# Decode attention: key chunks of 128 instead of 64, two-bank q·k sums, and A's output row as one 512-column strip

## The chip, the cores and the metric

The kernel runs on one core of a Trainium2 chip. The metric is the device time of one execution in microseconds (us). "PE" is the matmul engine, "DVE" VectorE, "ACT" ScalarE, "SP" the engine whose queue issues the loads; in the profile lines "PEld" is PE's loading of weights and "POOL" GpSimd. SBUF is the on-chip memory that holds the tiles, here over 128 partitions (128x8192 in the profile is 8192 elements in each); PSUM is the memory that PE sums into. A run's profile is of one of its executions, so its times belong to that execution alone. PE's granted clock is the share of full speed that the profile says it was given; in the records it is 0.50 or 1.00.

## The reference, cut to what matters

Two attention problems, A and B, one query token each, 32 heads of 128. A reads 16384 keys and values per head, B only the last 4096.

```
q      = x @ wq                                   # 512 -> 32 heads x 128
scores = einsum("bhqd,bhkd->bhqk", q, k) * 128**-0.5
p      = softmax(scores)
o      = einsum("bhqk,bhkd->bhqd", p, v)
out    = o.reshape(1, 1, 32 * 128) @ wo           # 4096 -> 512
# A: all 16384 keys; B: the last 4096; result: concatenate(a, b)
```

Every key and value is read once and used once: 335 MB of keys and values, 17 MB of weights.

## The kernel before

Keys come in loads of 8 MB (a tile of 128 partitions x 256 keys x 128 values, bf16; B's in two halves). DVE multiplies keys by q and folds the product once; PE sums on with identity matmuls; DVE reduces; ACT takes the exponential. All that goes by chunks of U keys.

```python
U = 64
KEYS = 256

def _mult(nc, cx, ch):                       # DVE: k *= q, in place
    ...
def _add(nc, cx, ch):                        # DVE: first half of d += second half
    k = ch.unit.load.kt[:, ch.k0 : ch.k0 + U, :]
    cx.o(nc.vector.tensor_tensor(
        out=k[:, :, 0 : DH // 2], in0=k[:, :, 0 : DH // 2], in1=k[:, :, DH // 2 : DH], op=ALU.add))

def _red(nc, cx, ch):                        # PE: 64 values -> 8, sums in PSUM
    W = 512 // U
    nb = DH // 2 // W
    ch.red = cx.red_pool.tile([P, U, W], F32, tag="red", name="red")
    for b in range(nb):
        cx.o(nc.tensor.matmul(ch.red[:, :, :], lhsT=cx.ident[:, :],
            rhs=ch.unit.load.kt[:, ch.k0 : ch.k0 + U, b * W : (b + 1) * W],
            start=(b == 0), stop=(b == nb - 1)))
    ...                                      # last chunk: the key buffer is free
```

The output rows come last. A's row of 512 is two strips of 256 columns (rows 0 and 32 of PSUM), B's likewise. PE works at two such strips together.

```python
def _out(nc, cx, st, j0, n):
    if j0 == 0:
        st.oc = ...                          # DVE copies the (P, J) columns out of PSUM
    w = st.DN // 2
    out = [o[r : r + 1, :] for o, r in zip(cx.out_ps, st.out_rows)]
    for j in range(j0, j0 + n):
        for x in range(2):
            cx.o(nc.tensor.matmul(out[x], lhsT=st.oc[:, j : j + 1],
                rhs=st.wo_t[:, j, x * w : (x + 1) * w], start=(j == 0), stop=(j == J - 1)))
    if j0 + n == J:
        ...                                  # DVE and ACT copy a half each; SP stores the row
```

The pools are laid out one after another in each SBUF partition:

```python
    cx.singles = pool("singles", 1)          # ident, place, csA, csB, masks, q, ...
    cx.small = pool("small", 1)
    cx.kt_pool = pool("kt", 2)               # two buffers of keys, 64 KB a partition each
    cx.vt_pool = pool("vt", 1)               # one buffer of values
    ...
    st.cs = cx.singles.tile([P, H, st.keys // U], F32, tag=f"cs{st.name}", name=f"cs{st.name}")
```

The softmax here doesn't subtract the row's maximum and nothing guards it: scores larger than these inputs give would overflow.

Of the kernel before, what the change touches and what calls it, by code (L numbers as in the profile page):

```python
# [8 lines left out]
F32 = mybir.dt.float32  # L9
BF16 = mybir.dt.bfloat16  # L10
P = 128
# [2 lines left out]
AX = mybir.AxisListType  # L14

DH = 128
U = 64
KEYS = 256
SCALE = 1.0 / math.sqrt(DH)

# [9 lines left out]
class _Order:  # L30


    def __init__(self, tc):
        self.tc = tc
# [27 lines left out]
class _Chunk:  # L62
    def __init__(self, unit, i):
        self.unit, self.i, self.k0 = unit, i, unit.k0 + i * U


class _Unit:


    def __init__(self, st, i, load, k0):  # L70
        self.st, self.i, self.R = st, i, st.R
        self.load, self.k0 = load, k0
        self.h0 = i * st.R
        self.chunks = [_Chunk(self, c) for c in range(st.keys // U)]
        self.stage = None
# [93 lines left out]
def _mult(nc, cx, ch):  # L169

    u = ch.unit
    k = u.load.kt[:, ch.k0 : ch.k0 + U, :]
    q = u.st.qall[:, u.i * DH : (u.i + 1) * DH]
    cx.o(nc.vector.tensor_tensor(  # L174
        out=k, in0=k,
        in1=q.rearrange("p (o d) -> p o d", o=1).broadcast_to([P, U, DH]),
        op=ALU.mult,
    ))


def _add(nc, cx, ch):
    k = ch.unit.load.kt[:, ch.k0 : ch.k0 + U, :]
    cx.o(nc.vector.tensor_tensor(  # L183
        out=k[:, :, 0 : DH // 2], in0=k[:, :, 0 : DH // 2], in1=k[:, :, DH // 2 : DH], op=ALU.add,
    ))


def _red(nc, cx, ch):
    W = 512 // U
    nb = DH // 2 // W  # L190
    ch.red = cx.red_pool.tile([P, U, W], F32, tag="red", name="red")
    for b in range(nb):
        cx.o(nc.tensor.matmul(  # L193
            ch.red[:, :, :],
            lhsT=cx.ident[:, :],
            rhs=ch.unit.load.kt[:, ch.k0 : ch.k0 + U, b * W : (b + 1) * W],
            start=(b == 0),
            stop=(b == nb - 1),
        ))
    if ch is ch.unit.load.chunks[-1]:  # L200
        cx.loads.release("kt")


def _softmax(nc, cx, ch):

    u = ch.unit
    R = u.R
    sc = cx.sc_pool.tile([P, U], F32, tag="sc", name="sc")
    cx.o(nc.vector.tensor_reduce(out=sc[:, :], in_=ch.red[:, :, :], axis=AX.X, op=ALU.add))  # L209
    ch.p = u.st.p_pool.tile([P, U // 4, R, 4], BF16, tag=f"p{u.st.name}", name="p_sb")  # L210
    for g in range(R):
        cx.o(nc.scalar.activation(  # L212
            out=ch.p[:, :, g, :],
            in_=sc[:, :].rearrange("p (t e) -> p t e", e=4),
            func=ACT.Exp,
            scale=SCALE,
            bias=u.st.off[:, g : g + 1],
            accum_out=u.st.cs[:, u.h0 + g, ch.i : ch.i + 1],
        ))
# [80 lines left out]
def _out(nc, cx, st, j0, n):  # L300
    J = st.wo.shape[0] // P
    if j0 == 0:
        st.oc = cx.singles.tile([P, J], BF16, tag=f"oc{st.name}", name=f"oc{st.name}")
        cx.o(nc.vector.tensor_copy(st.oc[:, :], st.oc_ps[:, 0:J]))  # L304
    w = st.DN // 2
    out = [o[r : r + 1, :] for o, r in zip(cx.out_ps, st.out_rows)]
    for j in range(j0, j0 + n):
        for x in range(2):
            cx.o(nc.tensor.matmul(  # L309
                out[x],  # L310
                lhsT=st.oc[:, j : j + 1],
                rhs=st.wo_t[:, j, x * w : (x + 1) * w],
                start=(j == 0),
                stop=(j == J - 1),
            ))
    if j0 + n == J:
        row = cx.accs_pool.tile([1, st.DN], BF16, tag="accs", name=f"row{st.name}")
        cx.o(nc.vector.tensor_copy(row[0:1, 0:w], out[0]))  # L318
        cx.o(nc.scalar.copy(row[0:1, w:], out[1]))
        cx.o(nc.sync.dma_start(out=cx.out[0, 0:1, st.at : st.at + st.DN], in_=row[0:1, :]))  # L320


# [1 line left out]
def kernel(  # L324
# [14 lines left out]
    nc = tc.nc  # L339
# [4 lines left out]
    cx = _Ctx()  # L344
    cx.o = _Order(tc)
    cx.out = out
    pool = lambda name, bufs, **kw: ctx.enter_context(tc.tile_pool(name=name, bufs=bufs, **kw))
# [3 lines left out]
    cx.kt_pool = pool("kt", 2)  # L351
    cx.vt_pool = pool("vt", 1)
    cx.accs_pool = pool("accs", 1)
    cx.sc_pool = pool("sc", 2)
    cx.p_poolA = pool("pA", 7)
    cx.p_poolB = pool("pB", 4)
    cx.red_pool = pool("red", 2, **PS)
    cx.psf_pool = pool("psf", 1, **PS)
    cx.pst_pool = pool("pst", 1, **PS)
# [5 lines left out]

    def problem(name, x, k_cache, v_cache, wq, wo, sk0, W, at):
        st = _Problem()
        st.name, st.x, st.wq, st.wo, st.at = name, x, wq, wo, at
        st.R, st.keys = (2, KEYS) if name == "A" else (4, KEYS // 2)
        assert st.R * W == P * st.keys  # L370
        st.DN = wo.shape[1]
        st.k_view = k_cache[0, :, sk0 : sk0 + W, :]
        st.v_view = v_cache[0, :, sk0 : sk0 + W, :]
        st.out_rows = (0, 32) if name == "A" else (64, 96)
        st.f_at = 0 if name == "A" else 32
        assert k_cache.shape[1] == 32
        st.p_pool = cx.p_poolA if name == "A" else cx.p_poolB
        n = KEYS // st.keys * st.R
        st.loads = [_Load(st, i) for i in range(k_cache.shape[1] // n)]
        st.units = [u for x in st.loads for u in x.units]  # L380
        return st

    stA = problem("A", A_x, A_k_cache, A_v_cache, A_wq, A_wo, 0, SkA, 0)
    stB = problem("B", B_x, B_k_cache, B_v_cache, B_wq, B_wo, SkB - WB, WB, A_wo.shape[1])

    loads = []
# [19 lines left out]
    for i, p in enumerate(pieces):  # L406
# [16 lines left out]
        out=cx.ident[:, :],  # L423
# [10 lines left out]
    w = cx.place_at + 2 * P  # L434
    cx.place = cx.singles.tile([64, w], BF16, tag="place", name="place")
    nc.gpsimd.affine_select(
        out=cx.place[:, :],
# [10 lines left out]
        out=rows[:, :], in_=cx.ident[:, :].rearrange("p (c w) -> p w c", w=32), axis=AX.X, op=ALU.add,  # L448
    )
    for st in (stA, stB):  # L450
# [5 lines left out]
            out=st.mask[:, :], in_=own.rearrange("p g e -> p e g"), axis=AX.X, op=ALU.add,  # L456
# [5 lines left out]
            out=st.sel[:, st.sel_at : st.sel_at + R],  # L462
            in_=own, axis=AX.X, op=ALU.add,
        )
    for st in (stA, stB):
        st.off = cx.singles.tile([P, st.R], F32, tag=f"off{st.name}", name=f"off{st.name}")
        nc.vector.tensor_reduce(
            out=st.off[:, :],
# [5 lines left out]
            out=st.off[:, :], in0=st.off[:, :], scalar1=-1.0, scalar2=1000.0,  # L474
# [6 lines left out]
    for acc in cx.acc:  # L481
# [1 line left out]
    cx.f_ps = cx.psf_pool.tile([P, 512], F32, tag="f", name="f_ps")  # L483
    stA.oc_ps = cx.pst_pool.tile([P, 512], F32, tag="ocp", name="oc_ps")
    stB.oc_ps = cx.acc[1]
    cx.out_ps = [
        cx.psout_pool.tile([P, A_wo.shape[1] // 2], F32, tag=f"out{i}", name=f"out{i}")
        for i in range(2)
    ]

    _spread_x(nc, cx, stA, 0, 0)
    _spread_x(nc, cx, stB, 1, stA.R * (A_wq.shape[0] // P) * P)
# [7 lines left out]
    def fin_pe():  # L500
        for u in fins:
            if u.stage == 1:
                _fin_fold(nc, cx, u)
                u.stage = 9
        fins[:] = [u for u in fins if u.stage != 9]

    def fin_dve():
        for u in fins:
            if u.stage == 0:
                _fin_pick(nc, cx, u)  # L510
                u.stage = 1

    def pv(load):
        for u in load.units:
            fin_pe()
            fin_dve()
            _pv(nc, cx, u)
            u.stage = 0
            fins.append(u)

    prev = None
    for i, x in enumerate(loads):
        for c, ch in enumerate(x.chunks):
            _mult(nc, cx, ch)
            if prev is not None:
                _softmax(nc, cx, prev)
            fin_pe()
            _add(nc, cx, ch)
            fin_dve()
            _red(nc, cx, ch)  # L530
            if i and c == min(i - 1, 2):
                pv(loads[i - 1])
            prev = ch
    _softmax(nc, cx, prev)
# [7 lines left out]
    for p in pieces:  # L542
        _out(nc, cx, *p)
# [30 lines left out]
```

## Time and profile before

| | before |
|---|---|
| time, median | 826.41 us (826.3 to 826.58, the first 3 runs) |
| DMA, mean over the span | 428 GB/s |
| DVE busy / ACT busy / PE busy | 612 / 78 / 380 us |
| last value load landed | 800.5 us |
| last piece of wo landed | 821.3 us |
| B's output matmuls end | 821.8 us |

The page's second part cuts the span in 40 slices; a digit is the busy share in tenths, and GB/s is what the DMA engines moved. Before:

```profile
DVE  2099896997479967799196959599557978699911
DMA  9999999999999999999999999999999999999997
GB/s 382 439 452 423 439 433 430 428 435 449 412 453 420 443 426 436 429 430 433 421 445 432 436 430 436 427 421 444 432 420 443 437 424 445 421 428 437 428 421 291
```

DMA never falls below nine tenths until the last slice; DVE does, again and again. The kernel is a stream of loads, and the engines keep up with it. From the page's first and fifth parts, before (in the fifth: busy us, mean ns of one, then idle time before it and what ended most of it):

```profile
PE 379.5 (46%) x2180; PEld 133.0 (16%) x2180; DVE 612.3 (74%) x316; ACT 78.4 (10%) x394; POOL 1.3 (0%) x9
L174 DVE TENSOR_TENSOR kt<-kt,qallA 128x8192 bf16<-128x8192 bf16 x64 | 282.7, 4417 | 129.1 <-DMA kt<-in_A_k_cache_dram 129.1
L183 DVE TENSOR_TENSOR kt<-kt 128x4096 bf16<-128x4096 bf16 x80 | 182.3, 2278 | 0.0
```

DVE sat 129 us waiting for A's keys. The end, from the timeline and the chain of waits (start us, length us, what), before:

```profile
800.55 3.37 PE L231 MATMUL acc<-vt,p_sb 128*16 128x512 bf16 x32 [7.83 <-DMA vt<-in_B_v_cache_dram]
807.24 5.18 PE L309 MATMUL out<-wo_t,ocA 128*1 128x256 bf16 x64 [0.25 <-DVE ocA L304]
815.24 1.91 PE L309 MATMUL out<-wo_t,ocB 128*1 128x256 bf16 x32 [2.82 <-DMA wo_t<-in_B_wo_dram]
817.71 1.04 PE L309 MATMUL out<-wo_t,ocB 128*1 128x256 bf16 x16 [0.56 <-DMA wo_t<-in_B_wo_dram]
818.94 1.03 PE L309 MATMUL out<-wo_t,ocB 128*1 128x256 bf16 x12 [0.19 <-DMA wo_t<-in_B_wo_dram]
821.39 0.38 PE L309 MATMUL out<-wo_t,ocB 128*1 128x256 bf16 x4 [1.42 <-DMA wo_t<-in_B_wo_dram]
...
790.79 30.56 DMA wo_t<-in_B_wo_dram
821.39 0.43 PE out L309 x4
821.86 0.42 DVE rowB L318
```

The first line is the last sum over values (p @ v), which waits for the last load of values. B's wo comes in five pieces, and PE stops four times to wait for one. The chain ends in the last piece: 1.42 us of waiting for it, four matmuls, a copy.

### The profile page before, as it was taken

Reading aid. Unit: us, or ns where it says so; the run is one execution under the profiler, and the core shown is the slowest. Engines: PE = TensorE matmul, PEld = TensorE weight load, DVE = VectorE, ACT = ScalarE, POOL = GpSimd, SP = SyncE. Lnnn points to the kernel's source line nnn. Section 1 sums busy time; section 2 is a strip of 40 time slices with the busy share of each in tenths; the row PEclk is TensorE's granted clock in tenths of the full one; section 3 lists DMA queues with packets and bytes.
Section 4 is the critical chain, followed back from the end, with each engine's and each line's share of the span. In section 5 each row is a group of like instructions: output and inputs, shape, how many; then the busy total and the mean of one; then the engine's idle time right before and its main releaser. Section 6 shows DMA issues by size and latency. Waiting matters only on the chain.

```text
span 824.5 us, 5323 instructions
## 1 busy us (share of the span) xinstructions
PE 379.5 (46%) x2180; PEld 133.0 (16%) x2180; DVE 612.3 (74%) x316; ACT 78.4 (10%) x394; POOL 1.3 (0%) x9
## 2 busy tenths in 40 slices
PE   3435563456063616255435435365515362535555
PEld 1111121112021202011111111121101120111123
DVE  2099896997479967799196959599557978699911
ACT  1100110111000100011010101011100100001200
POOL 0000000000000000000000000000000000000000
PEclk9766777676556856575657675776756685657579
DMA  9999999999999999999999999999999999999997
GB/s 382 439 452 423 439 433 430 428 435 449 412 453 420 443 426 436 429 430 433 421 445 432 436 430 436 427 421 444 432 420 443 437 424 445 421 428 437 428 421 291
DMA packets 8240, 352.67 MB, mean 428 GB/s; under 512 B 916, under 2 KB 920, under 8 KB 1304
## 3 DMA queue, kind: packets, MB, share of 16 engines
q1 hardware_dynamic: 8212, 352.33, 99.1%
q8 instruction: 17, 0.28, 0.1%
q14 instruction: 7, 0.06, 0.0%
q10 hardware_dynamic: 4, 0.00, 0.0%
HBM read 352.32 MB, written 0.00 MB: 427 GB/s over the span
## 4 chain that ended last, share of the span: by engine, by line
DMA 51%; DVE 33%; issue 8%; PE 7%; another core or an unknown queue 1%; SPq 0%; DVEq 0%
DMA kt<-in_A_k_cache_dram 43%; DVE kt L174 16%; DVE kt L183 12%; PE red L193 5%; DMA vt<-in_B_v_cache_dram 4%; DMA wo_t<-in_B_wo_dram 4%; DVE sc L209 4%; PE acc L231 3%; DVE s L251 1%; DVE acc L245 1%; SPq L123 0%; PE out L309 0%; DVE rowB L318 0%; DVEq L251 0%
## 5 line engine op out<-in xcount | busy, mean ns | idle before, releaser
L193 PE MATMUL red<-kt,ident 128*128 128x512 bf16 x640 | 255.2, 570 | 400.4 <-DVE kt L183 400.1
L174 DVE TENSOR_TENSOR kt<-kt,qallA 128x8192 bf16<-128x8192 bf16 x64 | 282.7, 4417 | 129.1 <-DMA kt<-in_A_k_cache_dram 129.1
L183 DVE TENSOR_TENSOR kt<-kt 128x4096 bf16<-128x4096 bf16 x80 | 182.3, 2278 | 0.0
L193 PEld LDWEIGHTS <-ident 128*128 128x128 bf16 x640 | 82.8, 131 | 559.3 <-issue 455.4
L231 PE MATMUL acc<-vt,p_sb 128*8 128x512 bf16 (+1 forms) x1280 | 90.9, 446 | 21.9 <-DMA vt<-in_A_v_cache_dram 12.8
L212 ACT ACTIVATE p_sb<-sc,offA 128x64 bf16<-128x64 f32 x128 | 43.5, 340 | 535.2 <-DVE sc L209 535.2
L174 DVE TENSOR_TENSOR kt<-kt,qallB 128x8192 bf16<-128x8192 bf16 x16 | 70.7, 4416 | 0.0
L209 DVE TENSOR_REDUCE sc<-red 128x64 f32<-128x512 f32 x80 | 54.5, 681 | 0.5 <-PE red L193 0.5
L231 PEld LDWEIGHTS <-p_sb 128*8 128x8 bf16 (+1 forms) x1280 | 33.0, 98 | 85.3 <-issue 62.2
L212 ACT ACTIVATE p_sb<-sc,offB 128x64 bf16<-128x64 f32 x64 | 21.5, 337 | 153.3 <-DVE sc L209 153.3
L245 DVE TENSOR_TENSOR acc<-acc,maskA 128x512 f32<-128x512 f32 x16 | 11.2, 698 | 28.3 <-PE acc L231 28.1
L245 DVE TENSOR_TENSOR acc<-acc,maskB 128x512 f32<-128x512 f32 x8 | 5.6, 696 | 30.8 <-PE acc L231 30.8
L212 ACT ACTIVATION_READ_ACCUMULATOR p_sb<-sc,offA 128x1 f32 x128 | 23.9, 186 | 0.0
L138 PE MATMUL q_ps<-wq_t,scr 128*128 128x512 bf16 x64 | 16.7, 427 | 5.0 <-DMA wq_t<-in_A_wq_dram 5.0
L251 DVE TENSOR_REDUCE s<-acc 128x128 f32<-128x512 f32 x24 | 16.6, 691 | 1.1
L212 ACT ACTIVATION_READ_ACCUMULATOR p_sb<-sc,offB 128x1 f32 x64 | 12.0, 187 | 0.0
L138 PEld LDWEIGHTS <-scr 128*128 128x128 bf16 x64 | 6.7, 107 | 14.5 <-issue 8.5
L318 DVE CAST rowB<-out 1x256 bf16<-1x256 f32 x1 | 0.4, 418 | 8.9 <-PE out L309 8.9
L309 PE MATMUL out<-wo_t,ocB 128*1 128x256 bf16 x64 | 4.3, 272 | 5.0 <-DMA wo_t<-in_B_wo_dram 5.0
L259 PE MATMUL f_ps<-s,selA 128*32 128x128 f32 x32 | 6.5, 285 | 0.0
L309 PE MATMUL out<-wo_t,ocA 128*1 128x256 bf16 x64 | 5.2, 338 | 0.3 <-DVE ocA L304 0.3
L110 DVE CAST scr<-xT 128x128 bf16<-128x128 f32 (+1 forms) x6 | 2.1, 458 | 3.7 <-PE xT L102 3.6
(46 smaller groups left out, 28.8 us busy)
## 6 DMA issues: line engine op xcount, KB each, us to landing
kt<-in_B_k_cache_dram SPq DMA_DIRECT2D x8, 4096.0 KB, 36.3
vt<-in_B_v_cache_dram SPq DMA_DIRECT2D x8, 4096.0 KB, 23.5
wq_t<-in_A_wq_dram SPq DMA_DIRECT2D x1, 4096.0 KB, 12.3
wq_t<-in_B_wq_dram SPq DMA_DIRECT2D x1, 4096.0 KB
wo_t<-in_A_wo_dram SPq DMA_DIRECT2D x2, 2048.0 KB, 22.5
wo_t<-in_B_wo_dram SPq DMA_DIRECT2D x1, 2048.0 KB, 26.9
wo_t<-in_B_wo_dram SPq DMA_DIRECT2D x1, 1024.0 KB, 28.9
wo_t<-in_B_wo_dram SPq DMA_DIRECT2D x1, 512.0 KB
```

Source lines behind the costliest of these rows:

```text
L110: cx.o(nc.vector.tensor_copy(st.xb[:, :, g, :].rearrange("p c (i r) -> p r c i", r=R)[:, g, :, :], xT[:, :].rearrange("p (c o) -> p c o", ...
L138: cx.o(nc.tensor.matmul(q_ps[:, :], lhsT=st.xb[:, c, g, :], rhs=w[:, g, j * (512 // DH) : (j + 1) * (512 // DH), :], start=(g == 0 and c = ...
L174: cx.o(nc.vector.tensor_tensor(out=k, in0=k, in1=q.rearrange("p (o d) -> p o d", o=1).broadcast_to([P, U, DH]), op=ALU.mult,))
L183: cx.o(nc.vector.tensor_tensor(out=k[:, :, 0 : DH // 2], in0=k[:, :, 0 : DH // 2], in1=k[:, :, DH // 2 : DH], op=ALU.add,))
L193: cx.o(nc.tensor.matmul(ch.red[:, :, :], lhsT=cx.ident[:, :], rhs=ch.unit.load.kt[:, ch.k0 : ch.k0 + U, b * W : (b + 1) * W], start=(b == ...
L209: cx.o(nc.vector.tensor_reduce(out=sc[:, :], in_=ch.red[:, :, :], axis=AX.X, op=ALU.add))
L212: cx.o(nc.scalar.activation(out=ch.p[:, :, g, :], in_=sc[:, :].rearrange("p (t e) -> p t e", e=4), func=ACT.Exp, scale=SCALE, bias=u.st.of ...
L231: cx.o(nc.tensor.matmul(u.acc[r : r + 4 * R, :], lhsT=ch.p[:, t % (U // 4), :, :], rhs=u.load.vt[:, k : k + 4, :], start=(t < 4), stop=(t ...
L245: cx.o(nc.vector.tensor_tensor(out=acc, in0=acc, in1=st.mask[:, :].rearrange("p (x o) -> p x o", o=1).broadcast_to([P, 4, DH]), op=ALU.mult,))
L251: cx.o(nc.vector.tensor_reduce(out=u.s[:, :], in_=acc.rearrange("p x d -> p d x"), axis=AX.X, op=ALU.add,))
L259: cx.o(nc.tensor.matmul(cx.f_ps[st.f_at : st.f_at + 32, 0:DH], lhsT=st.sel[:, at : at + 32], rhs=u.s[:, :], start=(u.i == 0), stop=(u.i == ...
L309: cx.o(nc.tensor.matmul(out[x], lhsT=st.oc[:, j : j + 1], rhs=st.wo_t[:, j, x * w : (x + 1) * w], start=(j == 0), stop=(j == J - 1),))
```

## The change

Its intent: half as many DVE and ACT instructions (an instruction has a fixed cost, 0.15 us by these two sizes: the product of twice the size takes 8686 ns and not twice 4417), and half as many output matmuls for A. Cut to its core (left out: the output rows' PSUM tile now comes from the pool of the sums):

```diff
-U = 64
+U = 128
+W = 8
@@ _red
-    for b in range(nb):                     # 8 matmuls into one bank
+    for k in range(0, U, n):                # n = 64: 2 x 8 matmuls into two banks
+        for b in range(nb):
@@ _out
-    w = st.DN // 2
-    out = [o[r : r + 1, :] for o, r in zip(cx.out_ps, st.out_rows)]
+    w = st.DN // st.cols
+    out = [cx.out_ps[r : r + 1, b, 0:w] for r, b in st.out_at]
...
-        for x in range(2):
+        for x in range(st.cols):
...
+        if st.cols == 2:
+            cx.o(nc.scalar.copy(row[0:1, w:], out[1]))
@@ pools
-    cx.sc_pool = pool("sc", 2)
-    cx.p_poolA = pool("pA", 7)
-    cx.p_poolB = pool("pB", 4)
+    cx.sc_pool = pool("sc", 1)
+    cx.p_poolA = pool("pA", 3)
+    cx.p_poolB = pool("pB", 2)
@@ problem
-        st.out_rows = (0, 32) if name == "A" else (64, 96)
+        st.out_at = ((0, 0),) if name == "A" else ((64, 0), (96, 1))
+        st.cols = len(st.out_at)
@@ main loop
-            if i and c == min(i - 1, 2):
+            if i and c == 0:                # p @ v of the load before: earlier
                 pv(loads[i - 1])
```

More of the change, by code (lines that the diff above doesn't have):

```diff
@@ L188, in _red @@
 def _red(nc, cx, ch):
-    W = 512 // U
+    n = 512 // W
     nb = DH // 2 // W
     ch.red = cx.red_pool.tile([P, U, W], F32, tag="red", name="red")
-    for b in range(nb):
-        cx.o(nc.tensor.matmul(
-            ch.red[:, :, :],
-            lhsT=cx.ident[:, :],
-            rhs=ch.unit.load.kt[:, ch.k0 : ch.k0 + U, b * W : (b + 1) * W],
-            start=(b == 0),
-            stop=(b == nb - 1),
-        ))
+    for k in range(0, U, n):
+        for b in range(nb):
+            cx.o(nc.tensor.matmul(
+                ch.red[:, k : k + n, :],
+                lhsT=cx.ident[:, :],
+                rhs=ch.unit.load.kt[:, ch.k0 + k : ch.k0 + k + n, b * W : (b + 1) * W],
+                start=(b == 0),
+                stop=(b == nb - 1),
+            ))
     if ch is ch.unit.load.chunks[-1]:
@@ L304, in _out @@
         cx.o(nc.vector.tensor_copy(st.oc[:, :], st.oc_ps[:, 0:J]))
-    w = st.DN // 2
-    out = [o[r : r + 1, :] for o, r in zip(cx.out_ps, st.out_rows)]
+    if cx.out_ps is None:
+        cx.out_ps = cx.red_pool.tile([P, 2, 512], F32, tag="red", name="out_ps")
+    w = st.DN // st.cols
+    out = [cx.out_ps[r : r + 1, b, 0:w] for r, b in st.out_at]
     for j in range(j0, j0 + n):
-        for x in range(2):
+        for x in range(st.cols):
             cx.o(nc.tensor.matmul(
@@ L318, in _out @@
         cx.o(nc.vector.tensor_copy(row[0:1, 0:w], out[0]))
-        cx.o(nc.scalar.copy(row[0:1, w:], out[1]))
+        if st.cols == 2:
+            cx.o(nc.scalar.copy(row[0:1, w:], out[1]))
         cx.o(nc.sync.dma_start(out=cx.out[0, 0:1, st.at : st.at + st.DN], in_=row[0:1, :]))
@@ L485 @@
     stB.oc_ps = cx.acc[1]
-    cx.out_ps = [
-        cx.psout_pool.tile([P, A_wo.shape[1] // 2], F32, tag=f"out{i}", name=f"out{i}")
-        for i in range(2)
-    ]
+    cx.out_ps = None
     _spread_x(nc, cx, stA, 0, 0)
```

## The prediction

> **What bounds the kernel now.** The DMA queue. The page shows the DMA at nine tenths or more in 39 of 40 slices; the queue table gives the loads 99.1% of the 16 engines' span, 352.3 MB at a mean of 428 GB/s. The table of stretches gives 430 to 434 GB/s from 42 to 710 us, with DVE at 74 to 80% of each stretch, so DVE is not the limit there. [...] so the stream has no headroom. The chain of waits ends in the load of B's wo, landed at 821.4, then 0.43 us of matmul, 0.42 us of eviction and the store.
>
> **What the change does.** VectorE: the product takes 4.42 us for 8192 elements and the add 2.28 us for 4096, so an instruction has a fixed cost of about 0.14 us (estimate from these two). Halving 240 instructions saves about 17 us of busy time: DVE from 612 to about 595 us. ScalarE: 96 exponentials (0.34 us) and 96 accumulator reads (0.19 us) go, the others grow a little: from 78 to about 50 us. PE: as many sum matmuls; A's output row in 32 matmuls of 512 columns, not 64 of 256.
>
> None of that is on the critical path: DVE already waits 129 us for A's keys (groups by line).
>
> **What could reach the path: when buffers come free.** Each 8 MB load lasts 19.4 us in the stream. The timeline of SyncE's issues, against the landing of the load before, leaves 5 to 8 us at the closest. After the change pv runs after the first half of a load (not three quarters), and a whole half's sums (16 matmuls, 7.1 us at half clock) go before it. By the trace's durations, steady state keeps 6 us or more at half clock; the start is tightest: load 2's keys issued near 76.5 us (73.7 now), V of load 1 near 97 us (88.0 now), against a stream that is filled until about 101 us. So 2 to 5 us remain: no gap.
>
> **The tail.** The last pv waits for the V data (800.5 us) as before, so A's output row starts at about 807 us as before. Its 64 matmuls took 5.2 us as two concurrent column strips; as one strip of 32 x 512 they should take about 7 us at full clock (0.21 us each, estimate from 8 sums in 1.90 us) and up to 13.7 at half clock (0.43 each). DVE's copy of the row grows from 0.41 to about 0.7 us. So B's output starts at about 815 us rather than 813, where it waits for wo until 815.2 anyway. Only if the clock stays halved from 807 to 821 does the tail grow, by up to 6 us.
>
> **Prediction.** 826.5 us; 825.3 to 828.5 holds it 8 times in 10. Faster by over 2%: 0.01; within 2%: 0.97; slower: 0.02.
>
> **Right if:** DMA stays at 9 in 39 slices and 430 GB/s; DVE busy falls to about 595 us and its idle before the product grows by about as much; the chain still ends in B's wo, landing at about 821 us; V of load 1 is issued 6 to 10 us later than now; A's output matmuls take 6 to 9 us.
>
> **Wrong if:** a gap opens in the stream (a slice below 9 near 100 us, or after every B load), each costing only its own length; or the last matmuls of B no longer wait for wo, because A's output ran at half clock.

"The stream has no headroom" rests on what stands before it, 39 slices of 40 at nine tenths and 99.1% of the 16 engines' span, and was the author's estimate. The forecast's 826.5 us is the 826.41 us of the kernel before with nothing taken off the stream and next to nothing added to the tail.

## The result, and the profile after

823.31 us (823.17 to 823.36, 4 runs) against 826.36 us (826.05 to 826.58, 4 runs). The ratio is 0.9963, 95% interval 0.9946 to 0.998: the mean time of one kernel's runs over that of the other's of the same rounds, so not quite the ratio of the medians. It is 3.05 us, 0.4%: "the same" at 2%, as predicted, but 2 us below the range given. So there is something to explain, and it is small.

The page after, parts one, two and five:

```profile
PE 341.5 (42%) x2148; PEld 127.6 (16%) x2148; DVE 603.5 (73%) x196; ACT 46.8 (6%) x201; POOL 1.3 (0%) x9
DMA  9999999999999999999999999999999999999997
L175 DVE TENSOR_TENSOR kt<-kt,qallA 128x16384 bf16<-128x16384 bf16 x32 | 278.0, 8686 | 135.1 <-DMA kt<-in_A_k_cache_dram 135.1
L184 DVE TENSOR_TENSOR kt<-kt 128x8192 bf16<-128x8192 bf16 x40 | 176.5, 4413 | 0.0
```

The engines have less to do: ACT 32 us less, DVE 9 us less. DVE's wait for keys grew from 129 to 135 us: of the 9 us that it gained, it waited 6 there. The end after, timeline and chain:

```profile
798.77 3.46 PE L233 MATMUL acc<-vt,p_sb 128*16 128x512 bf16 x32 [7.44 <-DMA vt<-in_B_v_cache_dram]
805.50 8.68 PE L313 MATMUL out_ps<-wo_t,ocA 128*1 128x512 bf16 x32 [0.25 <-DVE ocA L306]
814.22 0.68 DVE L322 CAST rowA<-out_ps 1x512 bf16<-1x512 f32 x1 [8.78 <-PE out_ps L313]
815.05 3.66 PE L313 MATMUL out_ps<-wo_t,ocB 128*1 128x256 bf16 x64 [0.87 <-DVE ocB L306]
...
756.14 42.58 DMA vt<-in_B_v_cache_dram
798.77 3.49 PE acc L233 x31
...
815.05 3.70 PE out_ps L313 x64
818.75 0.41 DVE rowB L322
```

Two things differ. Everything at the end comes earlier: the last values landed at 798.7 us instead of 800.5, so A's row starts 1.7 us earlier although the stream was full throughout in both. And B's 64 matmuls now run in one go, 815.05 to 818.71, behind A's row: nothing waits for wo any more. The last piece of wo landed at 818.2 us, not 821.3. Of the 3.1 us, 1.8 lie in the stream up to the last values and some 1.2 in the last 20 us.

Neither is in the engines. The trace's record of each DMA packet says more. One packet fills one partition (4096 packets of 64 KB for 32 loads of 128 partitions); this is its duration for A's loads between 90 and 790 us, worked out from those records:

```
64 KB packets, ns      10%    median   90%    mean
before                 2418   2422     2426   2424.1
after                  2418   2418     2418   2419.7
```

After the change nearly every packet takes exactly 2418 ns. Before, most take a few ns longer; 32 KB packets 1216 for 1213 ns, 16 KB packets 614 for 611 ns. By the medians it is some 3 to 4 ns a packet whatever its size. Summed over all packets of the loads (4096, 2304 and 384 of these sizes) and divided by 16 engines, the records give 816.9 us before and 815.4 after: 1.5 us of the 1.8 us of the stream. The rest is not accounted for packet by packet.

### The profile page after: what moved, and what is told of

The parts are those of the page before. It is cut to its first block, busy times and chain, and to the rows that moved or that the text cites. A ratio compares the mean times of both kernels' runs of the same rounds, so it can differ in the third digit from the quotient of the medians.

```text
span 821.3 us, 4921 instructions
## 1 busy us (share of the span) xinstructions
PE 341.5 (42%) x2148; PEld 127.6 (16%) x2148; DVE 603.5 (73%) x196; ACT 46.8 (6%) x201; POOL 1.3 (0%) x9
## 4 chain that ended last, share of the span: by engine, by line
DMA 54%; DVE 22%; PE 15%; issue 8%; SPq 0%; ACT 0%; DVEq 0%
DMA kt<-in_A_k_cache_dram 41%; PE red L195 11%; DVE kt L184 10%; DMA vt<-in_A_v_cache_dram 9%; DVE kt L175 8%; DMA vt<-in_B_v_cache_dram 5%; DVE sc L211 2%; PE acc L233 2%; PE out_ps L313 2%; DVE s L253 0%; DVE acc L247 0%; SPq L124 0%; DVE rowA L322 0%; SPq L167 0%; DVE rowB L322 0%
## 5 line engine op out<-in xcount | busy, mean ns | idle before, releaser
L195 PE MATMUL red<-kt,ident 128*128 128x512 bf16 x640 | 223.3, 526 | 417.7 <-DVE kt L184 417.7
L175 DVE TENSOR_TENSOR kt<-kt,qallA 128x16384 bf16<-128x16384 bf16 x32 | 278.0, 8686 | 135.1 <-DMA kt<-in_A_k_cache_dram 135.1
L184 DVE TENSOR_TENSOR kt<-kt 128x8192 bf16<-128x8192 bf16 x40 | 176.5, 4413 | 0.0
L233 PE MATMUL acc<-vt,p_sb 128*8 128x512 bf16 (+1 forms) x1280 | 83.0, 416 | 43.0 <-DMA vt<-in_A_v_cache_dram 35.5
L175 DVE TENSOR_TENSOR kt<-kt,qallB 128x16384 bf16<-128x16384 bf16 x8 | 69.5, 8682 | 0.0
L214 ACT ACTIVATE p_sb<-sc,offA 128x128 bf16<-128x128 f32 x64 | 25.2, 394 | 556.8 <-DVE sc L211 556.8
L211 DVE TENSOR_REDUCE sc<-red 128x128 f32<-128x1024 f32 x40 | 48.7, 1216 | 2.2 <-PE red L195 2.2
L214 ACT ACTIVATE p_sb<-sc,offB 128x128 bf16<-128x128 f32 x32 | 12.4, 390 | 163.7 <-DVE sc L211 163.7
L214 ACT ACTIVATION_READ_ACCUMULATOR p_sb<-sc,offA 128x1 f32 x64 | 11.9, 186 | 0.0
L313 PE MATMUL out_ps<-wo_t,ocA 128*1 128x512 bf16 x32 | 8.7, 438 | 0.3 <-DVE ocA L306 0.3
```

The source lines that it names most:

```text
L175: cx.o(nc.vector.tensor_tensor(out=k, in0=k, in1=q.rearrange("p (o d) -> p o d", o=1).broadcast_to([P, U, DH]), op=ALU.mult,))
L184: cx.o(nc.vector.tensor_tensor(out=k[:, :, 0 : DH // 2], in0=k[:, :, 0 : DH // 2], in1=k[:, :, DH // 2 : DH], op=ALU.add,))
L195: cx.o(nc.tensor.matmul(ch.red[:, k : k + n, :], lhsT=cx.ident[:, :], rhs=ch.unit.load.kt[:, ch.k0 + k : ch.k0 + k + n, b * W : (b + 1) * ...
L211: cx.o(nc.vector.tensor_reduce(out=sc[:, :], in_=ch.red[:, :, :], axis=AX.X, op=ALU.add))
L214: cx.o(nc.scalar.activation(out=ch.p[:, :, g, :], in_=sc[:, :].rearrange("p (t e) -> p t e", e=4), func=ACT.Exp, scale=SCALE, bias=u.st.of ...
L233: cx.o(nc.tensor.matmul(u.acc[r : r + 4 * R, :], lhsT=ch.p[:, t % (U // 4), :, :], rhs=u.load.vt[:, k : k + 4, :], start=(t < 4), stop=(t ...
```

## The experiments

Theories for the pace of the stream: **A**, the placement of the buffers: `cs` holds the sums of the exponentials, one column a chunk, so its size depends on U, and it lies ahead of the key and value buffers; halving `cs` moved the key and value buffers from byte 26240 of a partition to 25856 (these addresses are those the build assigns); 256 divides the second and not the first. **I**: fewer instructions disturb the stream less. **N**: noise between runs or chips. For the last 1.2 us: **T**, A's row in one strip. (In the texts written before the runs, P and S are names for "the gain lies in the stream" and "the difference is systematic".)

### First four

The control has no edit. `row_only` is the kernel before with A's row as in the change; `chunk_only` is the kernel after with

```diff
-        st.out_at = ((0, 0),) if name == "A" else ((64, 0), (96, 1))
+        st.out_at = ((0, 0), (32, 1)) if name == "A" else ((64, 0), (96, 1))
```

and `before_pad128` is the kernel before with 128 bytes of padding; "sc" is the tile of the sums that ACT takes the exponential of:

```diff
     cx.small = pool("small", 1)
+    cx.pad = pool("pad", 1)                 # 128 bytes, ahead of the keys
...
-    cx.sc_pool = pool("sc", 2)
+    cx.sc_pool = pool("sc", 1)              # room for the pad
...
+    nc.gpsimd.memset(cx.pad.tile([P, 64], BF16, tag="pad", name="pad")[:, :], 0.0)
```

> The kernel before, unchanged, as a control. Theory N (the 3 us are run-to-run or chip-to-chip noise in the pace of the DMA): time spreads by 1 us or more against the same kernel, and a second profile shows the 32 KB and 64 KB packets at another pace than 1216 and 2421 ns. Theory S (systematic): ratio 1.000 within 0.0007, 826.0 to 826.6 us, packets again longer than the kernel after's 1213 and 2418 ns, last wo piece landing near 821 us.

> The kernel before with only A's output row as one strip of 512 columns. Theory T (the gain lies in the tail, 1.2 us of it): about 825 us and a last wo landing within 0.3 us of the other pieces. Theory P (the gain lies in the pace of the stream, set by what the chunks changed): no gain, 826.0 to 826.8 us.

> The kernel after with A's output row back in two strips of 256 columns. Theory P: 823.0 to 823.6 us, packets at 1213 and 2418 ns as in the kernel after. Theory T: about 824.5 us, the last wo piece landing 1 us or more behind the others.

> The kernel before with 128 bytes a partition put ahead of the key and value buffers (their first byte then lies at an address that 256 divides, as in the kernel after; in the kernel before it doesn't), and one sc buffer to make room. Theory A (the placement of the buffers sets the packets' pace): packets at 1213 and 2418 ns, and 1.5 to 2 us less than before, about 824.5 us. Theory I (fewer instructions disturb the stream less): as before, 826.0 to 826.6 us.

| run | us, median (range) | ratio (95%) | 64 KB packets, mean ns | last values / last wo landed |
|---|---|---|---|---|
| aa_before | 826.31 (826.03 to 826.55) | 1.0 (0.9988 to 1.0013) | 2424.0 | 800.7 / 821.2 |
| row_only | 825.82 (824.95 to 826.19) | 0.9992 (0.9979 to 1.0004) | as before | 800.4 / 820.2 |
| chunk_only | 824.29 (824.03 to 824.44) | 0.9975 (0.9963 to 0.9988) | 2419.8 | 798.7 / 819.5 |
| before_pad128 | 824.39 (824.22 to 824.61) | 0.9978 (0.9964 to 0.9992) | 2420.2 | 798.6 / 819.3 |

N falls: the control repeats the time and the slower packets. Theory A is met to the tenth: 128 bytes of padding, and no other work removed (DVE busy 612.4 us, as before), give 1.84 us of the 3.05 and the packets of the kernel after. Rival I asked for 826 us here. The rest, 1.0 us, comes with A's row (after against `chunk_only`: their executions, 823.17 to 823.36 and 824.03 to 824.44 us, don't overlap, though the intervals of their ratios do). On the slow stream the same strip gave only 0.4 us and a wide range, though the last piece landed 1.0 us earlier. So `row_only` meets neither T (825 us) nor P (no gain). Its profile shows why: A's strip took 9.39 us, at a granted clock of 0.50 until 812.3 us, B's matmuls ran from 817.81 to 821.47 us, and PE was late, not the DMA.

### Placement, tested backwards, and its grain

The same padding in the kernel after moves its buffers to where we like: 384 bytes (with two strips, `chunk_only_pad384`) to exactly the address of the kernel before; 128, 256 and 64 bytes elsewhere.

> Chunks of 128 keys, A's row in two strips, and 384 bytes of padding, so that the key and value buffers start at exactly the address they have in the kernel before (26240 in a partition). Theory A (placement): packets back at 1216 and 2421 ns and 826.0 to 826.5 us: half as many VectorE and ScalarE instructions give nothing. Rival I (the instructions matter after all, placement only by chance): 824.3 us as without the padding.

> The kernel after with 128 bytes of padding: the buffers start at 25984, which 128 divides and 256 doesn't. Theory A with 256 bytes as the grain: packets at 1216 and 2421 ns and about 825 us. If the grain is 128 bytes or less, or placement is not the cause: 823.3 us.

> The kernel after with 256 bytes of padding: the buffers start at 26112, which 512 divides. Theory A with 256 bytes as the grain: no change, 823.3 us, packets 1213 and 2418 ns. If 512 is the grain: packets shorter still, and a few tenths of a us less.

> The kernel after with 64 bytes of padding: buffers at 25920, which 64 divides and 128 doesn't. If every start that 256 doesn't divide is as bad as another: packets 1216 and 2421 ns, about 825 us as with 128 bytes. If smaller grains cost more: longer packets than that and over 825.5 us.

| run | keys start at | 64 KB packets, 10% / median / 90% ns | us, median (range) |
|---|---|---|---|
| chunk_only_pad384 | 26240 = 102 x 256 + 128 | 2418 / 2422 / 2426 | 826.23 (826.09 to 826.25) |
| after_pad128 | 25984 = 101 x 256 + 128 | 2418 / 2421 / 2426 | 824.97 (824.68 to 825.26) |
| after_pad64 | 25920 = 101 x 256 + 64 | 2419 / 2420 / 2427 | 826.21 (825.81 to 826.46) |
| after_pad256 | 26112 = 102 x 256 | 2418 / 2418 / 2418 (all sizes as after) | 823.42 (823.01 to 824.25) |

`chunk_only_pad384` is the cleanest. It has the change's chunks, with these engines:

```profile
PE 339.9 (41%) x2180; PEld 128.1 (16%) x2180; DVE 603.1 (73%) x196; ACT 47.2 (6%) x202; POOL 1.5 (0%) x10
```

and its time is that of the kernel before, ratio 1.0 (0.9986 to 1.0013). So the halved DVE and ACT instructions are worth nothing here, and the 1.9 us came from where `cs`, half as large, let the buffers start. It also clears the single sc buffer that `before_pad128` needed: this kernel has it too and is slow. Both starts that 256 divides are fast, 26112, which 512 divides (823.42 us), and 25856, which it doesn't (823.31 us); 64 and 128 bytes off give packets of the same slower mean (64 KB: 2423.5 and 2423.6 ns). The further 1.2 us of `after_pad64` are not in its packets: in its profile A's row ran from 807.59 for 9.35 us, B's matmuls started at 817.81, and PE ended late, as in `row_only`.

What makes an unaligned start slower is not shown. The start that is off is where the loads write, in SBUF, and it costs 2 to 4 ns for a 64 KB packet by the medians (2420 to 2422 ns against 2418), and in the kernel before 3 ns for packets of 32 and 16 KB too, so the cost does not grow with the size. Nor is it there from the start: up to about 70 us the packets of the kernel before take as long as those of the kernel after (64 KB packets from 20 to 70 us: median 2418 ns in both, mean 2419.9 before, 2420.0 after), though the buffers lie where they always lie, and the extra comes only from there on (71 to 80 us: median 2422 before, 2418 after). Why stays open.

### The last microsecond: a fetch of instructions

In the records of the last microseconds there are other packets than the loads: 16 KB of instructions on a queue of their own, 17 in the whole run, one packet each, of 1.07 us in the mean before and 0.95 after. The records don't name the engine whose instructions they are; the texts written before the runs call them PE's, as a theory. What the page has for it: there are 17 before and after, though DVE's instructions fell from 316 to 196 and ACT's from 394 to 201, while PE's matmuls fell only from 2180 to 2148. From the same records (us; "others" are the loads' packets on the other engines, as far as the order of their ends shows):

```
                fetch from - to      last packets of the loads end        others done
before          818.82 - 819.92      820.68 820.76 820.84 820.92          819.8
chunk_only      816.72 - 817.64      818.85 818.93 819.01 819.09          817.9
after           817.50 - 818.58      817.76 817.79 817.81 817.84 817.89 817.97
```

In the kernels with two strips a row of packets, 0.08 us apart, ends after all others. They stood behind the fetch: followed back in `chunk_only`, each begins where the one before it ends, down to a packet that begins at 817.63 us, the end of the fetch, and the fetch begins at 816.72 us, where that engine's packet before it ends. PE then waits for the last pieces, here in `chunk_only`:

```profile
818.93 0.38 PE L313 MATMUL out_ps<-wo_t,ocB 128*1 128x256 bf16 x4 [1.35 <-DMA wo_t<-in_B_wo_dram]
819.56 0.38 PE L313 MATMUL out_ps<-wo_t,ocB 128*1 128x256 bf16 x4 [0.24 <-DMA wo_t<-in_B_wo_dram]
```

In the kernel after, the fetch runs on when every load has ended. Theory **F**: the fetch holds up one engine by 1 us, the last piece of wo lands that much later, and the one-strip row moves the fetch out of the way. First guess at why: the fetch comes a fixed number of instructions from the end of PE's program. `before_pad128_tail` adds instructions at that end:

```diff
     for p in pieces:
         _out(nc, cx, *p)
+    for _ in range(24):                      # nobody reads it
+        cx.o(nc.tensor.matmul(cx.f_ps[0:1, 200:201], lhsT=cx.ident[:, 0:1], rhs=cx.ident[:, 0:1], ...))
```

> The padded kernel before with 24 tiny matmuls of one column after the last output matmul; nobody reads them. Theory F (one DMA engine's last packets are held up for 1 us by a fetch of 16 KB of PE's instructions, which comes when PE is some 35 instructions from the end of its program): the fetch moves behind the last wo piece, that piece lands at about 818.3 us and not 819.3, the time falls from 824.4 to about 823.4 us. Rival C (the fetch comes at a fixed place of the program counted from its beginning, or the late piece has another cause): the last piece still lands 1 us behind, 824.4 us or more.

824.30 us (824.19 to 824.34), fetch at 817.05 us, last piece at 819.5 us: that guess was wrong. Second guess: it comes a fixed number of instructions from the beginning, and the strip, with 64 PE instructions less (32 matmuls and 32 weight loads on the page), puts it later. `after_more_pe` puts 32 such matmuls behind the q projection of the kernel after.

> The kernel after with 32 tiny matmuls of one column (64 PE instructions) early, while PE waits for the first keys; nobody reads them. Theory F2 (the fetch of PE's instructions comes at a fixed place of the program; A's row in one strip has 64 instructions less, so the last fetch comes only when its DMA engine has moved its last wo packets): with the 64 instructions back, the fetch comes before 817 us, packets end behind it, the last wo piece lands at about 819.2 us and the time rises from 823.3 to about 824.2 us. Rival R (the strip gains because PE or the eviction ends sooner): no change, 823.3 us, last landing 818.2 us.

824.21 us, but from 823.08 to 825.27; the profile fell on the execution of 823.08, with the fetch at 817.57 us and nothing behind it. The two next runs hold B's matmuls back by 8 or 20 unused matmuls of 512 columns between A's and B's output matmuls of `before_pad128`:

> The padded kernel before, two strips, with 8 matmuls of 512 columns (nobody reads them) between A's and B's output matmuls: 1.7 us of PE, over before B's wo arrives at 813.3 us. A control for the added instructions: B starts as before, the fetch of PE's instructions comes near 817 us, packets end behind it, last piece at about 819.3 us, 824.3 us. If added instructions alone move the fetch: another time.

> The same with 20 such matmuls, 4.3 us of PE, so that B's output matmuls start at about 815.2 us and not 813.3. Theory F3 (A's row in one strip gains because it holds B's matmuls back, and with them the fetch of PE's instructions, until the DMA engine that serves it has moved its last wo packets): fetch at 817.5 us or later, nothing ends behind it, last piece at 818.2 us, 823.3 us although PE has more to do (824.2 us in executions where the clock stays halved for longer). Rival R2 (the strip itself, fewer instructions or fewer evictions, gives the gain): 824.3 us or more.

> The kernel after with 64 more PE instructions early, once more, since its profile showed the fetch at 817.6 us and no late piece while four of its five times were 824.2 us or more. F2 (those 64 instructions bring the fetch forward): a profile at 824.2 us shows packets ending behind a fetch before 817 us. F3 (only the start of B's matmuls counts): in a profile at 824.2 us B's matmuls start at 816 us and end at 819.7 us, as in the kernel after's own 824.2 us executions, and the last piece lands at 818.2 us.

`before_pad128_hold8` did as a control should: 824.36 us (824.27 to 824.59), last piece at 819.5 us. `before_pad128_hold20` missed: 824.34 us (824.30 to 824.59). It held B's matmuls to 815.5 us, but the fetch came at 815.62 us, earlier than without them, and packets ended behind it up to 819.10 us. Its time is the one that rival R2 forecast, but the run didn't create the condition it was to test; why the fetch came earlier was not shown. It does show that holding B back is not enough in itself: B began as late as in the kernel after, and the last piece still landed at 819.5 us.

```profile
815.47 0.38 PE L309 MATMUL out<-wo_t,ocB 128*1 128x256 bf16 x4
819.53 0.38 PE L309 MATMUL out<-wo_t,ocB 128*1 128x256 bf16 x4 [0.22 <-DMA wo_t<-in_B_wo_dram]
```

`after_more_pe_again`: 824.11 us (823.30 to 824.94). Its profile (824.94 us) shows something else. Stretches of 2 us from 79, 81 and 83 us moved only 386, 372 and 410 GB/s (worked out from the packets' records; 434 around them), the last values landed at 800.7 us, 2 us late, and the last piece of wo at 820.2 us: load 2's keys had been issued at 77.22 us, and a gap opened. In the kernel after they were issued at 75.75 us, in the first profile of this kernel at 76.39, without a gap. So 64 more instructions do not bring the fetch forward; what the spread of this kernel's times is made of in each execution is left open.

The last pair keeps PE's program as it is and holds B's matmuls back by what they read: one DVE addition ahead of the copy that they wait for (`dve_hold`), or behind it (`dve_work`), both in `before_pad128`.

```diff
     if j0 == 0:
         st.oc = ...
+        if st.name == "B":                   # into keys that are done with
+            k = st.loads[-1].kt
+            cx.o(nc.vector.tensor_tensor(out=k[:, 0:108, 0:64], in0=k[:, 0:108, 0:64],
+                in1=k[:, 0:108, 64:128], op=ALU.add))
         cx.o(nc.vector.tensor_copy(st.oc[:, :], st.oc_ps[:, 0:J]))
```

> The padded kernel before, two strips, with one VectorE add of 6912 elements (into keys that are done with; 3.7 us) ahead of the copy that B's output matmuls wait for: they start at about 815.1 us and not 813.3, PE's program is unchanged[...]. Theory F3 (what counts is that the fetch of PE's instructions comes after its DMA engine has moved the last wo packets; the strip does it by holding B back): fetch at 817.4 us or later, nothing ends behind it, last piece at 818.2 us, 823.3 us, or 824.2 us where B starts at 816 us. Rival R2 (the strip itself): 824.4 us, last piece at 819.3 us.

> Control: the same VectorE add, but behind that copy, so that it holds nothing back. Both theories: B starts at 813.3 us, fetch near 817 us, packets end behind it, last piece at 819.3 us, 824.4 us.

```
                fetch from - to      last packets of the loads end        last wo landed   us, median (range)
dve_work        816.76 - 817.69      818.72 818.80 818.88 818.96          819.4            824.17 (824.03 to 824.32)
dve_hold        817.56 - 818.52      817.74 817.78 817.82 817.82          818.1            825.96 (824.94 to 826.96)
```

With two strips and the same PE program, holding B back by 3 us moved the fetch behind the loads, and the last piece landed 1.3 us earlier. With `before_pad128_hold20`, where B was held back and the fetch was not, this leaves the fetch as what the landing follows; R2 had forecast 819.3 us for `dve_hold`. That half of F is shown. The time did not follow, for a reason that the timeline of `dve_hold` shows, `dve_work` below it for comparison:

```profile
812.28 3.74 DVE L306 TENSOR_TENSOR kt<-kt 128x6912 bf16<-128x6912 bf16 x1
816.18 6.08 PE L314 MATMUL out<-wo_t,ocB 128*1 128x256 bf16 x64 [4.27 <-DVE ocB L309]
```

```profile
813.20 1.91 PE L314 MATMUL out<-wo_t,ocB 128*1 128x256 bf16 x32 [2.77 <-DMA wo_t<-in_B_wo_dram]
819.42 0.38 PE L314 MATMUL out<-wo_t,ocB 128*1 128x256 bf16 x4 [0.23 <-DMA wo_t<-in_B_wo_dram]
```

PE had stood idle for 4.27 us, and B's 64 matmuls then took 6.08 us where they take 3.66 in the kernel after. The strip holds B back nearly as long (to 815.05 us) and keeps PE busy meanwhile. PE's granted clock in `dve_hold` was 0.50 from 814.3 to 821.2 us, over most of these matmuls, and 1.00 over the 3.66 us in the kernel after; that the idle time before them lowered it is not shown. That an earlier landing also saves its time is seen only with the strip (`chunk_only` against the kernel after), not in this pair.

### Placement and strip, without the chunks

`row_pad128` is `row_only` with the 128 bytes of padding and one sc buffer: the kernel before, with 64-key chunks.

> The kernel before, chunks of 64 keys as they were, with 128 bytes of padding (one sc buffer to make room) and A's output row in one strip. If placement and the strip are the whole of the change: 823.3 us like the kernel after, within 0.3 us, packets 1213 and 2418 ns, last landing 818.2 us, though VectorE keeps its 612 us. If the chunks add anything: 823.6 us or more.

> The kernel after, unchanged, beside the three others on the same chip: 823.2 to 823.5 us.

`row_pad128`: 823.21 us (823.0 to 824.17), ratio 0.9966 (0.9953 to 0.9978), last wo piece at 818.1 us. Beside it on the same chip, the kernel after: 823.29 us (823.12 to 824.34), 0.9968 (0.9955 to 0.998). `row_pad128` has all of the gain and none of the chunks:

```profile
PE 388.5 (47%) x2148; PEld 134.1 (16%) x2148; DVE 612.8 (75%) x316; ACT 77.9 (9%) x393; POOL 1.4 (0%) x10
```

Both have executions at 823.2 and at 824.2 us. The profile of the kernel after's second set fell on one at 824.17 us: the strip took 9.43 us instead of 8.68, B's matmuls ran from 816.09 to 819.75 us, and the last piece had landed at 818.2. There PE is late, not the DMA. The granted clock says why: in the first profile of the kernel after it was 0.50 until 808.8 us and 1.00 from there, in this one 0.50 until 810.6 us, so more of the strip ran at half clock. With these executions in the mean, the strip's gain over `chunk_only` is some 0.6 us and not 1.0 (ratio 0.9968 against 0.9975).

```profile
805.79 9.43 PE L313 MATMUL out_ps<-wo_t,ocA 128*1 128x512 bf16 x32 [0.25 <-DVE ocA L306]
816.09 3.66 PE L313 MATMUL out_ps<-wo_t,ocB 128*1 128x256 bf16 x64 [0.87 <-DVE ocB L306]
```

No run beat the kernel after; `row_pad128` equals it.

## Why the prediction was right or wrong

- **DMA bounds it, and of the DVE and ACT savings "none of that is on the critical path": right.** `chunk_only_pad384` has all of the savings and a ratio of 1.0.
- **"The stream has no headroom": wrong, and the first step that failed.** 39 slices of 40 at nine tenths and 430 to 434 GB/s through the middle of the span looked like the end. But 0.2% was left in the packets: their sum fell from 816.9 to 815.4 us, and the last values landed 1.8 us earlier, more than the 1.2 us between the forecast of 826.5 us and the lower end of its range. The prediction looked at when buffers come free, not at where they lie. The diff halves a tile that lies ahead of them; the build's addresses could have shown that they move. What that is worth, 3 to 4 ns a packet, had to be measured.
- **"The chain still ends in B's wo, landing at about 821 us", and A's strip can only lengthen the tail: wrong, the second step.** A's strip took 8.7 us (about 7 at full clock, 6 to 9 allowed), and B started at 815.05 us (about 815 predicted); that this start agrees is luck, since the strip began 1.7 us earlier than predicted and took 1.7 us longer than 7. And wo landed at 818.2 us: 1.8 us earlier by the packets' pace, and 1.3 by the fetch that no longer stands ahead of the last packets. The sign that the prediction named for a longer tail, B's last matmuls no longer waiting for wo, came with a shorter one. The prediction took the time of the last landing as given by bytes alone; that one engine did other work in front of it was in the trace of before (queue table, "instruction") and was not asked about.
- **"So 2 to 5 us remain: no gap": right for the kernel after, but too generous.** Load 2's keys were issued at 75.75 us (76.5 predicted), and an issue at 77.22 us in a sister kernel did cost a gap. Since an issue at 76.39 us opened none, the slack was 0.6 to 1.5 us. The prediction also read DVE as busy for 74 to 80% of each stretch from 42 us on; in the stretch that matters here, 42 to 120 us, it was 74.3 of 78 us, 95%. V of load 1 was issued at 93.19 us, 5.1 us later than before (6 to 10 predicted).
- **"DVE busy falls to about 595 us": mis-sized, 603.5.** The sums of the durations fell as predicted (product, add and reduction by 17 us together), but most instructions overlapped the one before by about 0.08 us, which busy time counts once: 20.1 us of overlap before, 11.5 after. ACT: 46.8 us (about 50 predicted).

## What to carry to other kernels

When a load stream fills the DMA engines (99.1% of their span here), look at the start address of its buffers in a partition: one that 256 divides was worth 0.2% here, and any small tile ahead of it can undo it unseen. At the end of a stream the last piece lands with the last of its packets, so see what stood in front of them: here a fetch of instructions of about 1 us, and the landing was 1.3 us later with it than without (`dve_work` against `dve_hold`). A fix that puts more work on PE there can make PE the late one, as in the executions at 824.2 us. And a gain that comes with a change need not come from its intent: put the layout back, keep the intent, and measure again.
